# TensorE in the program's order for the mixed batches, with preparation in eight spaced stages, sums in the V products' banks and u transposed early

**Chip, cores, metric.** One Trainium2 chip, one core. The metric is the device time of one launch in microseconds (us), median of several runs. All runs used here were fast (granted TensorE clock 0.98 to 1.00).

## The reference

Hash attention, then a Fourier mixing layer with a two-layer channel network. Cut to what matters:

```python
# q, k, v: (4, 8, 768, 64); proj: (64, 6); w_ch1: (512, 2048); w_ch2: (2048, 512)
q_bucket = sum((q @ proj > 0) * 2 ** arange(6)); k_bucket = ...
scores = where(q_bucket == k_bucket, q @ k.T / 8, -1e9)
x = softmax(scores) @ v                       # -> (4, 768, 512)
u = x + real(fft(fft(x, axis=1), axis=2))
un = (u - mean(u)) / sqrt(var(u) + 1e-6)
out = u + maximum(un @ w_ch1, 0) @ w_ch2
```

## The kernel before

Two heads are worked as a pair n (16 pairs, four per batch). A pair has six key blocks c; one step weighs two query halves g against block c, exponentiates on ACT, masks on DVE, and multiplies the block before by V. The mixing of batch b-1 is a generator of 68 steps (Fourier products cs, A and B; h and o of the channel network), drawn between the attention steps of batch b. Names in the profile: sc scores, oo the product with V, sum the row sums, trq/trk transposed q/k, bits/qb/kb hash bits, un the transposed u.

```python
def pt(shape, name):                   # general tiles: 2 PSUM slots while attention runs
    ...
    return ps_1.tile(shape, F32, tag="ps", name=name)

def prepare(n):                        # yields: after q, after k, after bits, after qb and kb
    ...

def weigh(n, g, c):
    ps = ps_sc.tile([P, 2, 512], F32, tag="sc", name=f"sc{n}_{g}_{c}")
    ...
    for h, rows in enumerate(heads):   # head 0: array rows 0-63, head 1: rows 64-127
        nc.tensor.matmul(ps[:, h, 0:HALF], kt[rows, ks], qt[rows, qs], ...)
    nc.scalar.activation(pk[:, :, 0:HALF], ps[:, :, 0:HALF], AF.Exp, scale=SCALE)
    if kb is not None:
        for h in range(2):
            nc.vector.scalar_tensor_tensor(pk[:, h, 0:HALF], qb[:, h, qs],
                kb[:, h, c : c + 1], pk[:, h, 0:HALF], op0=ALU.is_equal, op1=ALU.mult)
    return pk

def scale(n, oos, accs):
    nc.vector.tensor_copy(vs, oos[0][:, HALF : HALF + 1])
    for g, xg in enumerate(halves):
        nc.scalar.activation(xg, oos[g][:, 0:HALF], AF.Identity, bias=vs)
    for g, xg in enumerate(halves):
        ps = pt([P, HALF], f"sum{n}_{g}")
        ...                            # sum matmuls, then a chain of six DVE operations
# attention of batch 0: every engine keeps the program's order (manual_schedule)
# batches 1 to 3: the framework's scheduler orders every engine by its own time model
```

## Time and profile before

| | us |
|---|---|
| median of 4 runs (lowest to highest) | 1219.55 (1218.6 to 1220.84) |
| span of the profiled run | 1218.6 |
| TensorE busy / idle in the span | 1182.9 / 35.7 |
| DVE, ACT busy | 635.4, 347.0 |

The main lines stand in the prediction below. Read them so: TensorE is busy 97% of the span, so the kernel is as long as TensorE's instruction stream. A record of a 384-column matmul lasts about 490 ns, but the next one starts 322.5 ns later, so "busy" says little. The measure used throughout is the **excess**: the time from each record's start to the next one's, summed over a stretch, less what the same records need at their undisturbed spacing (322.5 ns for 384 columns, 429 for 512, 109 for 128; two halves of the array side by side count half each, the four quarters of bits a quarter each). It holds waits, changes of array shape, half-array matmuls that run without their partner.

### The profile page before, as it was taken

The numbers are of one execution on the slowest core, as the hardware profiler recorded it, in microseconds if no ns is written. First come the engines' busy times: TensorE is split into PE (matmuls) and PEld (weight loads), VectorE is DVE, ScalarE is ACT, GpSimd is POOL, SyncE is SP. The second block draws the span as 40 slices with busy tenths as digits, with TensorE's granted clock in tenths as the row PEclk, the third lists the DMA queues.
The fourth block names the chain that finished last, engine by engine and source line by source line (L and its number), as shares of the span: only waits on it lengthen the run. The fifth ranks groups of instructions, "written<-read, shape, count | busy, mean of one in ns | idle before, by whom it ended". The sixth has DMA issues, their size and how long they took to land. (4 is left out here: it accounts for less than half of the span.)

```text
span 1218.6 us, 11905 instructions
## 1 busy us (share of the span) xinstructions
PE 1182.9 (97%) x4617; PEld 596.3 (49%) x4617; DVE 635.4 (52%) x1202; ACT 347.0 (28%) x612; POOL 57.6 (5%) x128
## 2 busy tenths in 40 slices
PE   7999899999999999999999999999999999999997
PEld 4444364444444456454445445554445546654555
DVE  5889869753374547545446555655445753211110
ACT  7877356532132122222222213222122210000000
POOL 1000001000000010000000010000000000001001
PEclk9999999899999999999999999999999999999999
DMA  9522124201010010100101011010000000000000
GB/s 277 156 65 45 44 87 147 83 14 43 9 26 14 22 38 6 27 13 22 35 22 27 1 31 35 1 39 1 22 17 1 1 10 18 1 1 17 9 9 20
DMA packets 82896, 44.24 MB, mean 36 GB/s; under 512 B 76816, under 2 KB 76944, under 8 KB 82832
## 3 DMA queue, kind: packets, MB, share of 16 engines
q1 hardware_dynamic: 75600, 23.61, 8.0%
q0 software_dynamic: 5664, 19.40, 4.9%
q8 instruction: 38, 0.62, 0.2%
q10 hardware_dynamic: 1568, 0.39, 0.2%
q14 instruction: 26, 0.21, 0.1%
HBM read 37.10 MB, written 6.29 MB: 36 GB/s over the span
## 5 line engine op out<-in xcount | busy, mean ns | idle before, releaser
L1018 PE MATMUL h<-x,w 128*128 128x384 f32 x1024 | 346.3, 494 | 4.8 <-ACT qt L530 2.4
L1049 PE MATMUL o<-w,h 128*128 128x512 f32 (+1 forms) x800 | 339.9, 578 | 0.0
L1018 PEld LDWEIGHTS h<-x,w 128*128 128x128 f32 x1024 | 192.2, 191 | 150.8 <-issue 13.1
L805 DVE SCALAR_TENSOR_TENSOR pk<-qb,kb,pk 128x384 f32<-128x384 bf16 x264 | 151.2, 615 | 184.0 <-ACT pk L802 183.8
L1049 PEld LDWEIGHTS o<-w,h 128*128 128x128 f32 x800 | 148.3, 190 | 169.5 <-issue 160.3
L802 ACT ACTIVATE pk<-sc 128x768 f32<-128x768 f32 x192 | 148.4, 809 | 217.8 <-PE sc L796 178.7
L796 PE MATMUL sc<-qt,kt 64*128 64x384 f32 x768 | 187.3, 507 | 0.0
L816 PE MATMUL oo<-pk,vn 128*64 128x385 f32 (+1 forms) x768 | 145.0, 499 | 0.0
L876 DVE TENSOR_TENSOR acc<-acc,pk 128x768 f32<-128x768 f32 x128 | 120.4, 955 | 9.2 <-ACT pk L802 7.6
L1027 ACT ACTIVATE h<-h 128x384 f32<-128x384 f32 x64 | 31.4, 490 | 281.3 <-PE h L1018 281.2
L1025 DVE TENSOR_SCALAR h<-h 128x384 f32<-128x384 f32 x64 | 35.5, 554 | 143.0 <-PE h L1018 142.9
L796 PEld LDWEIGHTS sc<-qt,kt 64*128 64x128 f32 x768 | 76.6, 186 | 65.9 <-issue 44.3
L1055 DVE SCALAR_TENSOR_TENSOR u<-o,rs,u 128x512 f32<-128x512 f32 (+1 forms) x25 | 18.2, 729 | 165.8 <-PE o L1049 118.3
L816 PEld LDWEIGHTS oo<-pk,vn 128*64 128x64 f32 x768 | 46.6, 136 | 87.3 <-issue 82.5
L1036 ACT COPY u<-un 128x512 f32<-128x512 f32 x24 | 14.0, 586 | 127.3 <-PE un L1034 127.3
L1042 POOL TENSOR_SCALAR rs<-mv 128x1 f32<-128x1 f32 x24 | 7.7, 323 | 593.4 <-DVE mv L1040 588.4
L903 POOL DMA_DIRECT2D out_dram<-u x33 | 19.9, 603 | 316.4 <-DVE u L1055 255.7
L964 PE MATMUL cs<-ch,z 128*128 128x128 f32 (+3 forms) x192 | 31.1, 314 | 2.6 <-DVE kt L528 1.4
L964 PEld LDWEIGHTS cs<-ch,z 128*128 128x128 f32 x192 | 27.5, 191 | 10.1 <-DVE kt L528 3.1
L971 ACT COPY F<-cs 128x257 f32<-128x257 f32 (+1 forms) x32 | 11.1, 374 | 74.7 <-PE cs L964 74.7
L876 DVE TENSOR_TENSOR acc<-pk,pk 128x768 f32<-128x768 f32 x32 | 30.0, 951 | 2.0 <-ACT pk L802 1.7
L828 ACT ACTIVATE x<-oo,vs 128x384 f32<-128x384 f32 x32 | 16.8, 577 | 41.3 <-DVE vs L825 41.3
(107 smaller groups left out, 805.7 us busy)
## 6 DMA issues: line engine op xcount, KB each, us to landing
zraw<-in_moe_w_ch_dram POOLq DMA_DIRECT2D x21, 512.0 KB, 4.5
vn<-in_v_dram SPq DMA_DIRECT2D x32, 192.0 KB, 3.3
qn<-in_q_dram SPq DMA_DIRECT2D x31, 192.0 KB, 3.2
kn<-in_k_dram SPq DMA_DIRECT2D x31, 192.0 KB, 3.2
out_dram<-u POOLq DMA_DIRECT2D x15, 256.0 KB, 2.4
out_dram<-u POOLq DMA_DIRECT2D x18, 128.0 KB, 2.5
fraw<-in_moe_w_ch_dram SPq DMA_DIRECT2D x4, 512.0 KB, 9.2
fraw<-in_moe_w_ch_dram POOLq DMA_DIRECT2D x4, 512.0 KB, 4.5
```

Of the source, the lines that this page charges most:

```text
L796: nc.tensor.matmul(ps[:, h, 0:HALF], kt[rows, ks], qt[rows, qs], start=kb is not None, stop=True,)
L802: nc.scalar.activation(pk[:, :, 0:HALF], ps[:, :, 0:HALF], AF.Exp, scale=SCALE)
L805: nc.vector.scalar_tensor_tensor(pk[:, h, 0:HALF], qb[:, h, qs], kb[:, h, c : c + 1], pk[:, h, 0:HALF], op0=ALU.is_equal, op1=ALU.mult,)
L816: nc.tensor.matmul(oos[g][h * D : (h + 1) * D, 0:w], nat["v", n][:, c, h, :], pk[g][:, h, 0:w], start=(c == 0), stop=(c == NT - 1),)
L876: nc.vector.tensor_tensor(accs[g], first[g][:, :, 0:HALF] if c == 1 else accs[g], new[g][:, :, 0:HALF], op=ALU.add,)
L903: nc.gpsimd.dma_start(out[b, s0 : s0 + 2 * w - 1 : 2, cols], src[at : at + w, cols])
L964: nc.tensor.matmul(ps[:, pc + 2 * lo : pc + 2 * hi - 1 : 2], z[:, cp, pc, par, t * P : (t + 1) * P], ch[:, cp, pc, lo:hi], start=(cp == 0) ...
L1018: nc.tensor.matmul(ps, w1[:, c, fc * P : (fc + 1) * P], x[:, c, g * HALF : (g + 1) * HALF], start=(c == 0), stop=(c == NDC - 1),)
L1025: nc.vector.tensor_scalar(hr, ps, 0.0, None, op0=ALU.max)
L1027: nc.scalar.activation(hr, ps, AF.Relu)
L1049: nc.tensor.matmul(ps, hs[fc][:, j * P : (j + 1) * P], w2[:, fc, cols], start=(fc == 0), stop=(fc == NFC - 1),)
L1055: nc.vector.scalar_tensor_tensor(u[:, cols], ps, rs, u[:, cols], op0=ALU.mult, op1=ALU.add)
```

## The change

The intent: the automatic order pulls the two heads of a score tile apart, and TensorE then runs half empty. So TensorE is tied to the program's order in batches 1 to 3, and the program is rearranged so that this order has few waits: preparation in eight smaller stages with mixing steps between them, the sums' PSUM tiles taken from the V products' two banks so that mixing keeps both general slots, A and B by parity so that a tile is free sooner, u transposed one step before it is needed. Cut to its core (the moved blocks of the batch loop and the new indentation are left out):

```diff
@@ prepare @@
                         ps.rearrange("p c t -> p (c t)"), act,
                     )
+                yield
             ts[nm] = tt
-            yield
             norm(n, io, tn)
...                                   # (the same for bits; and a yield after each qb)
@@ scale @@
-            ps = pt([P, HALF], f"sum{n}_{g}")
+            ps = ps_o.tile([P, HALF], F32, tag="o", name=f"sum{n}_{g}")
@@ attention @@
+    PARTS = 3
+            if c == 0:
+                oos += [ps_o.tile([P, 512], F32, tag="o", ...) for g in range(2)]
             values(n, c, pk, oos)
...
-                if c > 0:
-                    next(ahead, None)
+                for _ in range(PARTS - 1):
+                    yield
+                    if c > 0:
+                        next(ahead, None)
                 yield
+        yield
         while pending:
             finish()
@@ mix @@
-            pa, pb = (pt([P, HALF + 1], f"{nm}{b}_{j}") for nm in "AB")
             for par in range(2):
+                ps = pt([P, 2, NK], f"AB{b}_{j}_{par}")
...                                   # 128 additions of 192 columns for 64 of 384
                 hs.append(hr)
+                if fc == NFC - 2:
+                    nxt = across(b, GT * g)      # transposes u, its mean and variance
                 yield
@@ the batch loop @@
-    LEFT = 8
+    LEFT = 12
-    for b in range(B):
+    with tc.manual_schedule(engines={ET.PE}):
+        for b in range(B):
...
+        roomy[0] = True
+        for _ in range(2 + NT + NDC):
+            next(other)
...                                   # then the check of norms and the load of its flag
```

More of the change, by code (lines that the diff above doesn't have):

```diff
@@ L741, in prepare @@
                         nc.vector.tensor_scalar(bits, bits, BIG, None, op0=ALU.mult)
-                yield
+                    yield
             preps[n] = ts["q"], ts["k"], qk, None
@@ L856, in finish @@
             n, c, pk, oos, accs = pending.pop(0)
+            if c == 0:
+                oos += [
+                    ps_o.tile([P, 512], F32, tag="o", name=f"oo{n}_{g}") for g in range(2)
+                ]
             values(n, c, pk, oos)
@@ L866, in attention @@
             ahead = prepare(n + 1) if n + 1 < NPAIR * B else iter(())
-            oos = [ps_o.tile([P, 512], F32, tag="o", name=f"oo{n}_{g}") for g in range(2)]
+            oos = []
             accs = [wt([P, 2, HALF], F32, "t3", f"acc{n}_{g}", 4) for g in range(2)]
@@ L884, in attention @@
                     next(half, None)
-                if c > 0:
-                    next(ahead, None)
+                for _ in range(PARTS - 1):
+                    yield
+                    if c > 0:
+                        next(ahead, None)
                 yield
+        yield
         while pending:
@@ L945, in fold, with across @@
             yield
+    def across(b, T):
+        x = xs[b]
+        ps = pt([P, NDC, P], f"un{b}_{T}")
+        for c in range(NDC):
+            nc.tensor.transpose(ps[:, c, :], x[:, c, T * P : (T + 1) * P], ident)
+        u = wt([P, DM], F32, "u", f"u{b}_{T}", 2)
+        nc.scalar.copy(u, ps.rearrange("p c n -> p (c n)"))
+        bs = wt([P, 6], F32, "bs", f"bs{b}_{T}")
+        nc.vector.bn_stats(bs, u)
+        mv = wt([P, 2], F32, "mv", f"mv{b}_{T}")
+        nc.vector.bn_aggr(mv, bs)
+        rs = wt([P, 1], F32, "rs", f"rs{b}_{T}")
+        nc.gpsimd.tensor_scalar(rs, mv[:, 1:2], 1e-6, None, op0=ALU.add)
+        nc.gpsimd.tensor_tensor(rs, rs, mhalf, op=ALU.pow)
+        return u, rs
     def mix(b):
@@ L987, in mix @@
         for j in range(NDC):
-            pa, pb = (pt([P, HALF + 1], f"{nm}{b}_{j}") for nm in "AB")
             for par in range(2):
-                cols = slice(par * NK, HALF + 1 if par else NK)
-                for k, ps in enumerate((pa, pb)):
+                ps = pt([P, 2, NK], f"AB{b}_{j}_{par}")
+                n = NK - par
+                cols = slice(par * NK, par * NK + n)
+                for k in range(2):
                     for t in range(2):
                         nc.tensor.matmul(
-                            ps[:, cols], F[:, par, k, t, j * P : (j + 1) * P],
+                            ps[:, k, 0:n], F[:, par, k, t, j * P : (j + 1) * P],
                             sq[:, t, k, cols], start=(t == 0), stop=(t == 1),
                         )
-            for i in range(2):
-                u = x[:, j, i * HALF : (i + 1) * HALF].rearrange("p (r n) -> p r n", r=2)
-                for ps, op in (
-                    (pa, ALU.add), (pb, ALU.subtract if (j < 2) ^ i else ALU.add)
-                ):
-                    if i == 0:
-                        f = ps[:, 0 : 2 * NK - 1]
-                        f = bass.AP(f.tensor, f.offset, [f.ap[0], [NK, 2], [1, HW]])
-                    else:
-                        f = ps[:, HW : HALF + 1]
-                        f = bass.AP(f.tensor, f.offset, [f.ap[0], [HW, 2], [-1, HW]])
-                    nc.vector.tensor_tensor(u, u, f, op=op)
+                for i in range(2):
+                    at = i * HALF + par * HW
+                    u = x[:, j, at : at + HW]
+                    for k in range(2):
+                        f = ps[:, k, 0:HW]
+                        if i == 1:
+                            f = turned(ps[:, k], n - 1, HW)
+                        op = ALU.subtract if k and (j < 2) ^ i else ALU.add
+                        nc.vector.tensor_tensor(u, u, f, op=op)
             yield
@@ L1031, in mix @@
                 T = GT * g + j
-                ps = pt([P, NDC, P], f"un{b}_{T}")
-                for c in range(NDC):
-                    nc.tensor.transpose(ps[:, c, :], x[:, c, T * P : (T + 1) * P], ident)
-                u = wt([P, DM], F32, "u", f"u{b}_{T}", 2)
-                nc.scalar.copy(u, ps.rearrange("p c n -> p (c n)"))
-                bs = wt([P, 6], F32, "bs", f"bs{b}_{T}")
-                nc.vector.bn_stats(bs, u)
-                mv = wt([P, 2], F32, "mv", f"mv{b}_{T}")
-                nc.vector.bn_aggr(mv, bs)
-                rs = wt([P, 1], F32, "rs", f"rs{b}_{T}")
-                nc.gpsimd.tensor_scalar(rs, mv[:, 1:2], 1e-6, None, op0=ALU.add)
-                nc.gpsimd.tensor_tensor(rs, rs, mhalf, op=ALU.pow)
+                u, rs = nxt
                 w = DM // 2 if b == B - 1 and T == NT - 1 else DM
@@ L1053, in mix @@
                         if fc % 4 == 3:
+                            if fc == NFC - 5 and j < GT - 1:
+                                nxt = across(b, T + 1)
                             yield
@@ L1084, in _main @@
         for i, _ in enumerate(attention(0)):
-            if i % 5 < 4:
+            if i % PARTS == PARTS - 1 and i // PARTS % 5 < 4:
                 next(other, None)
@@ L1095, in _main @@
             nc.scalar.copy(means[-1][1], average(f))
-    for b in range(B):
-        if b > 0:
-            wait = 0
-            if b == 1:
-                next(other)
-                next(other)
-                wait = 2
-            steps, done = NPAIR * NT - wait, 2 if b == 1 else 0
-            for i, _ in enumerate(attention(b), 1):
-                if b == 1 and i == 2:
-                    for f, avg in means:
-                        centre(f, avg)
-                while done * steps < (MIX - LEFT) * (i - wait):
-                    next(other)
-                    done += 1
-        if b == B - 1:
-            roomy[0] = True
-            ms = const.tile([P, 3], F32, tag="ms", name="ms")
-            nc.vector.tensor_reduce(ms[:, 0:2], norms, axis=AX.X, op=ALU.max)
-            nc.vector.tensor_reduce(ms[:, 2:3], strange, axis=AX.X, op=ALU.max)
-            ps = pt([1, 3, P], "norms_t")
-            for io in range(3):
-                nc.tensor.transpose(ps[:, io, :], ms[:, io : io + 1], ident)
-            mt = const.tile([1, 5], F32, tag="mt", name="mt")
-            nc.vector.tensor_reduce(mt[:, 0:3], ps, axis=AX.X, op=ALU.max)
-            nc.vector.tensor_tensor(mt[:, 3:4], mt[:, 0:1], mt[:, 1:2], op=ALU.mult)
-            nc.vector.tensor_scalar(
-                mt[:, 4:5], mt[:, 3:4], (SAFE / SCALE) ** 2, None, op0=ALU.is_gt
-            )
-            fl = const.tile([1, 1], I32, tag="fl", name="fl")
-            nc.vector.scalar_tensor_tensor(
-                fl, mt[:, 2:3], 0.0, mt[:, 4:5], op0=ALU.is_gt, op1=ALU.max
-            )
-            large = nc.values_load(fl[0:1, 0:1], min_val=0, max_val=1)
@@ new lines, in _main @@
+    with tc.manual_schedule(engines={ET.PE}):
+        for b in range(B):
+            if b > 0:
+                wait = 0
+                if b == 1:
+                    next(other)
+                    next(other)
+                    wait = 2 * PARTS
+                steps, done = NPAIR * NT * PARTS - wait, 2 if b == 1 else 0
+                for i, _ in enumerate(attention(b), 1):
+                    if b == 1 and i == wait:
+                        for f, avg in means:
+                            centre(f, avg)
+                    goal = (MIX - LEFT) * (i - wait) / steps
+                    if i > NPAIR * NT * PARTS:
+                        goal = MIX - LEFT + 4
+                    while done < goal:
+                        next(other)
+                        done += 1
+            for _ in other:
+                pass
+            other = mix(b)
+            if b == 0:
+                other = after(2 + NT, other, weights(w2, moe_w_ch2))
+        roomy[0] = True
+        for _ in range(2 + NT + NDC):
+            next(other)
+        ms = const.tile([P, 3], F32, tag="ms", name="ms")
+        nc.vector.tensor_reduce(ms[:, 0:2], norms, axis=AX.X, op=ALU.max)
+        nc.vector.tensor_reduce(ms[:, 2:3], strange, axis=AX.X, op=ALU.max)
+        ps = pt([1, 3, P], "norms_t")
+        for io in range(3):
+            nc.tensor.transpose(ps[:, io, :], ms[:, io : io + 1], ident)
+        mt = const.tile([1, 5], F32, tag="mt", name="mt")
+        nc.vector.tensor_reduce(mt[:, 0:3], ps, axis=AX.X, op=ALU.max)
+        nc.vector.tensor_tensor(mt[:, 3:4], mt[:, 0:1], mt[:, 1:2], op=ALU.mult)
+        nc.vector.tensor_scalar(
+            mt[:, 4:5], mt[:, 3:4], (SAFE / SCALE) ** 2, None, op0=ALU.is_gt
+        )
+        fl = const.tile([1, 1], I32, tag="fl", name="fl")
+        nc.vector.scalar_tensor_tensor(
+            fl, mt[:, 2:3], 0.0, mt[:, 4:5], op0=ALU.is_gt, op1=ALU.max
+        )
+        large = nc.values_load(fl[0:1, 0:1], min_val=0, max_val=1)
@@ L1135, in _main @@
         for _ in other:
             pass
-        other = mix(b)
-        if b == 0:
-            other = after(2 + NT, other, weights(w2, moe_w_ch2))
-    for _ in other:
-        pass
     return large
```

## The prediction

> **What bounds the kernel now.** I read the page first, then the busy time in stretches, then TensorE's timeline, then the list of waits.
>
> ```profile
> PE 1182.9 (97%) x4617; PEld 596.3 (49%) x4617; DVE 635.4 (52%) x1202; ACT 347.0 (28%) x612; POOL 57.6 (5%) x128
> PE   7999899999999999999999999999999999999997
> PEclk9999999899999999999999999999999999999999
> ```
>
> TensorE is busy 97% of the span at an almost full granted clock (mean 0.994); nothing else comes near. So the end is set by the length of TensorE's instruction stream, and idle time can give back at most 1218.6 - 1182.9 = 35.7 us. About 8 us of that is the start, before the first loads have landed, and 7.7 us the last store after the last matmul; neither is touched.
>
> ```profile
> 0.00:150.70 150.70, 133.72 (x713) 61.29 (x713) 123.54 (x228) 101.65 (x187) 6.49 (x28) 0.99 0.43 117
> 150.70:441.60 290.90, 285.86 (x1085) 140.84 (x1085) 166.34 (x321) 98.27 (x173) 19.74 (x35) 0.99 0.17 48
> 441.60:737.40 295.80, 292.68 (x1121) 143.24 (x1120) 159.48 (x300) 70.10 (x118) 10.77 (x21) 1.00 0.09 22
> 737.40:998.00 260.60, 257.73 (x1022) 128.25 (x1021) 143.93 (x263) 61.90 (x103) 7.00 (x15) 1.00 0.06 15
> 998.00:1218.60 220.60, 212.87 (x683) 122.67 (x680) 42.07 (x91) 15.06 (x32) 13.57 (x29) 0.99 0.03 10
> ```
>
> These stretches (length, then busy time of PE, PEld, DVE, ACT, POOL) are cut where each batch's first mixing product (cs) runs: roughly attention of batch 0; attention 1, 2 and 3 each mixed with the Fourier and channel work of the batch before; and batch 3's mixing alone. In the three middle stretches (847 us) TensorE is idle only 11 us. But busy time counts a matmul's whole record, so it hides a stream that is spread out. What is spread shows in the timeline:
>
> ```profile
> 491.19 1.56 PE L796 MATMUL sc<-qt,kt 64*128 64x384 f32 x8
> 492.68 1.51 PE L816 MATMUL oo<-pk,vn 128*64 128x385 f32 x8
> 494.02 1.46 PE L833 MATMUL sum<-acc,ones 128*64 128x384 f32 x8
> ...
> 515.43 0.91 PE L796 MATMUL sc<-qt,kt 64*128 64x384 f32 x2
> 516.27 1.51 PE L816 MATMUL oo<-pk,vn 128*64 128x385 f32 x8
> 517.71 0.87 PE L708 MATMUL trk<-ident,kn 128*128 128x128 f32 x6
> 518.51 0.91 PE L796 MATMUL sc<-qt,kt 64*128 64x384 f32 x2
> ```
>
> A score tile (sc) is two heads, each on 64 rows of the array, each f32 product recorded as two passes: four records. At 491.19 two whole tiles, eight records, take 1.49 us until the next kind starts: the heads run side by side. At 515.43 one head's two records take 0.84 us alone, and the other head follows at 518.51, again alone. The program issues both heads together; the automatic order pulled them apart. Batch 0's attention, which already keeps program order, shows almost only whole groups.
>
> I took TensorE's records of the three middle stretches in order of start. Spacing inside a run of one shape is constant: 322.5 ns for 384 columns, 429 for 512, 109 for 128, and half of 322.5 per record where two halves of the array run together. Summed at that spacing (sc and oo counted as paired) the three stretches need 747 us; they take 847. The 100 us of excess are 11 us of waits and 89 us in which a record is "busy". There are 344 runs of one array shape. Excess per run (median): full array 0.20 us; oo 0.15; bits 0.14; qb/kb 0.10; sc 0.20 with whole tiles, 0.52 with a head alone. By kind: full 123 runs, 28.1 us; sc 115 runs, 46.1; oo 72 runs, 11.0; the rest 3.6. Of the 115 sc runs 66 contain a head alone.
>
> **What the Trainium skill says.** "TensorE: Matmul & The Clock Gate", Part 3, The mechanism: matmuls on different row groups of the array run concurrently, and matmuls keep strict issue order. The trace agrees: paired records start 7 ns apart, and a head whose partner comes later does not catch up. "TensorEngine Tiling (Array Packing)", Key Properties: changing the tiling mode drains TensorE. The trace puts a number on it: about 0.1 us at the end of a run and 0.05 to 0.1 at the next one's start. "Perfetto Trace Analysis", Identifying the Most-Contended Engine: matmul busy share does not tell how near a kernel is to its limit, because matmuls are pipelined; here 97% busy hides the 89 us.
>
> **The change, part by part.**
>
> *TensorE in program order for batches 1 to 3.* Every step then is: two whole score tiles, the V product, then mixing and preparation. 24 steps times 3 batches = 72 rounds, each with one sc run, one oo run and at least one full-array run. Preparation adds runs: eleven pairs (n = 5 to 15) use bits, qb twice and kb, each of another array shape. With the mixing steps between them (56 over 72 places, 0.78 a place) I count about 34 more full runs and 33 short ones. Sum: sc 72 x 0.20 = 14.5; oo 72 x 0.15 = 11; full 106 x 0.21 = 22.3; bits 11 x 0.14 = 1.5; qb and kb 33 x 0.10 = 3.2; together 52.5 us in place of 88.8. **Saved: 36 us**, all on the bounding engine. The 11 us of waits belong to the old order and go too; new ones come below.
>
> *Sums in the V products' two banks.* The sum matmul follows the V product at once (316 ns after its last record in nearly all pairs). It now needs a bank that is read first by DVE (vs, 0.15) and by ACT (x, 0.58).
>
> ```profile
> 493.05 1.15 DVE L805 SCALAR_TENSOR_TENSOR pk<-qb,kb,pk 128x384 f32<-128x384 bf16 x2 [3.70 <-ACT pk L802]
> 494.11 0.15 DVE L825 COPY vs<-oo 128x1 f32<-128x1 f32 x1
> ...
> 494.30 1.05 ACT L828 ACTIVATE x<-oo,vs 128x384 f32<-128x384 f32 x2 [0.58 <-DVE vs L825]
> ```
>
> Here the first of ACT's two ends at 494.88; the sum started at 494.02. It would have started at 494.93, 0.9 us late; the second sum then finds its bank free. Where no mask work stands before vs (at 995.0, for one) it is about 0.45 us. Twelve pairs: **about +9 us**. In batch 0 the vector engine is full of weight conversion: for the first pair vs came at 43.06 and the sum had run at 41.73, so there the wait is 1.5 to 2.2 us, and the reciprocal chain on DVE is delayed with it. Four pairs, nearly 8 us; DVE and TensorE are both near their limits there, so I take **+6 us**.
>
> *Preparation in eight stages.* No matmul more or less. It puts a transposition of 0.65 us between mixing steps that share two PSUM slots: the mixing step after it needs the slot of the one before it, whose eviction (0.49 on ACT, 0.55 on DVE) hardly fits into 0.65 us, and DVE's mask and accumulate burst in a step (4 x 0.56 + 2 x 0.95 = 4.1 us) sometimes stands before it. I take 0.4 us a pair for twelve pairs: **+5 us**.
>
> *A and B by parity.* The same matmuls; 128 vector additions of 192 columns at about 0.35 us (the z rows with 192 columns took 352 ns) for 64 of 0.55: DVE +10 us in all. Per step of A and B DVE then needs 2.8 us against TensorE's 2.6; with the mask work beside it DVE leads for two attention steps in each of three batches, and TensorE in strict order can't go past: **+5 us**. Alone at the end (batch 3) the lag stays below the 1.9 us for which the first three quarters of an h product run: 0.
>
> *u transposed early.* Moves 12.2 us of transpositions by one step; they waited for nothing: 0. *The flag (norms) later, in TensorE's order:* one short chain, **+1 us**. First h products after A and B, bits before qb where no mixing step falls between: **+2 us**.
>
> Sum: -36 - 11 + 9 + 6 + 5 + 5 + 1 + 2 = -19; 1219.3 - 19 = **1200 us**, a gain of 1.6%.
>
> **Rivals.**
>
> *Order pays in full.* If DVE takes vs before the masks and the slots come free in time, the new waits shrink to some 8 us in all: 1219 - 47 + 8 = about 1180. For it: slices at 52% DVE and 28% ACT leave room, and constants such as twelve steps kept back look tried out. Against: the dependency of the sum on ACT cannot be ordered away.
>
> *New waits eat the gain.* Strict order with two slots stalls at every preparation stage (48 transpositions, 0.6 us each, as in the waits of h for "ACT qt" now: 2.4 us in 4 times) and 2 us per sum: 29 + 24 + 10 = 63 us for 47 saved, about 1235. For it: the automatic order exists to fill such holes. Against: batch 0, in program order, had about 9 us of waits after its start. Something half-way, near 1212, is likelier.
>
> *Vector engine becomes the bound in cs and A/B stages.* It was 22 of 30 us busy at 450 to 480. 15 us more instead of my 5: 1210.
>
> **Range and chances.** The 36 us are counted from measured runs and I trust them to 5 us. The 28 us of new waits may be 12 to 40. So 1184 to 1212. A gain over 2% needs less than 1194.9, 5 us below my figure with a spread of about 10: 0.30. Slower by 2% needs 1243.7, 72 us of new waits: 0.04. Within 2%: 0.66.
>
> **What would show it.** Right: in the middle stretches every sc run has eight f32 records and about 72 sc runs are left; the mean time from sc to the next start per tile falls; sum now waits for "ACT x", about 0.9 us, 16 times; the last 212 us stretch is unchanged. Wrong: heads still apart (then the order was not the cause); sum not waiting; waits of h or o for "ACT h", "DVE h" or "DVE acc" in tens of us; batch 0 longer by over 10 us.

## The result

The changed kernel takes 1246.79 us (4 runs, 1244.88 to 1248.58) against 1219.55: ratio 1.0222, 95% interval 1.0204 to 1.0241. It is **slower by 2.2%**; forecast were 1200 us and 1184 to 1212. (A ratio here is the mean time of one kernel's fast runs over that of the other's of the same rounds, so not quite the ratio of the medians.) The output is correct.

The changed kernel's page, to set beside the first fence of the prediction:

```profile
span 1242.9 us, 11964 instructions
PE 1163.0 (94%) x4617; PEld 586.4 (47%) x4617; DVE 650.3 (52%) x1266; ACT 345.7 (28%) x612; POOL 54.6 (4%) x128
PE   7988887999999998999998999899999999999997
```

The same 4617 matmuls are *busy* 20 us less and *idle* 80 us in place of 36. Its stretches, cut at the first cs of each batch as before (length; busy PE, PEld, DVE, ACT, POOL; clock; DMA):

```profile
0.00:156.30 156.30, 134.07 (x708) 59.92 (x708) 123.71 (x228) 102.27 (x187) 6.47 (x28) 0.99 0.41 113
156.30:456.80 300.50, 282.30 (x1088) 139.28 (x1088) 167.84 (x334) 96.31 (x172) 18.04 (x37) 0.98 0.16 46
456.80:756.30 299.50, 283.18 (x1122) 139.29 (x1120) 164.74 (x316) 69.49 (x119) 9.88 (x22) 1.00 0.09 22
756.30:1046.70 290.40, 277.51 (x1084) 137.31 (x1083) 161.26 (x310) 63.64 (x106) 9.49 (x20) 1.00 0.06 14
1046.70:1242.90 196.20, 185.91 (x620) 110.60 (x618) 32.74 (x78) 13.97 (x30) 10.70 (x23) 0.99 0.03 10
```

Idle time stands now in every stretch with attention: 18 us in the second, where there were 5. (The lengths of the last two can't be compared: some 27 us of o products of batch 2 moved from the last to the one before it.) From here on the middle is cut from batch 0's first cs to the last oo record, in every kernel.

Who TensorE waited for (total us, times, longest), the changed kernel:

```profile
PE sum L834 <- ACT x L829: 17.1, 16, 2.5
PE AB L1023 <- DVE x L1036: 9.3, 7, 3.4
PE h L1045 <- DVE h L1052: 6.2, 6, 1.8
PE cs L993 <- DVE kt L528: 5.1, 3, 2.8
...
PE AB L1023 <- DVE F L1006: 3.2, 2, 1.6
PE trq L708 <- ACT qt L530: 3.1, 2, 1.6
PE h L1045 <- DVE fl L1164: 2.6, 1, 2.6
PE trq L708 <- DVE h L1052: 2.3, 3, 1.3
```

Two of these in the timeline. First a sum; then an h product between two transpositions:

```profile
505.97 1.56 PE L797 MATMUL sc<-qt,kt 64*128 64x384 f32 x8
507.46 1.51 PE L817 MATMUL oo<-pk,vn 128*64 128x385 f32 x8
509.71 1.51 PE L834 MATMUL sum<-acc,ones 128*64 128x384 f32 x8 [0.74 <-ACT x L829]
511.15 2.20 PE L1045 MATMUL h<-x,w 128*128 128x384 f32 x6
...
534.34 1.82 DVE L885 TENSOR_TENSOR acc<-acc,pk 128x768 f32<-128x768 f32 x2
534.84 0.49 PE L708 MATMUL trk<-ident,kn 128*128 128x128 f32 x3
536.08 0.55 DVE L1052 TENSOR_SCALAR h<-h 128x384 f32<-128x384 f32 x1
536.69 2.85 PE L1045 MATMUL h<-x,w 128*128 128x384 f32 x8 [1.36 <-DVE h L1052]
```

At 505.97 the score tiles are whole, eight records at a time, in every step: this part works as forecast. But the sum starts 1.22 us after the last V record in place of 0.32. At 534 the vector engine accumulates until 536.1, only then evicts the h tile before the transposition, and the next h product, which needs that slot, stands still 1.36 us although its operands have long been there. An idle interval also costs more than its idle time: the record before it covers some 0.17 us in which the next could have started (0.91 us lost at the sum, 0.74 of them idle), and the first record after it takes about 0.1 us more.

One more thing is in these traces. The granted clock falls to 0.50 for stretches of about 3.4 us, and the same 16 matmuls then take 1.6 us more:

```profile
182.50 4.47 PE L1023 MATMUL AB<-sq,F 128*128 128x193 f32 x16 [3.39 <-DVE x L1036]
...
197.92 2.88 PE L1023 MATMUL AB<-sq,F 128*128 128x193 f32 x16
```

The middle of the changed kernel has three such stretches (at 182.4, 202.9 and 230.2 us), each at the end of a wait or within 1 us of it. That the wait brings the lower clock is not shown by any run. Estimated as half of TensorE's busy time in such stretches, they cost the middle about 5 us in the changed kernel, 3 in the kernel before, 15 in order_only, 8.5 in sums_back and stages_paired, 3.4 in tiles_glued and none in attention_glued. They are a small part of the 25 us lost (2 us), but not of order_only's loss. They also differ between runs of one kernel: the changed kernel read 0.994 at 1244.88 us and 0.991 at 1248.58.

### The profile page after: what moved, and what is told of

It is laid out like the page before. It is cut to its first block, busy times and chain, and to the rows that moved or that the text cites. A ratio compares the mean times of both kernels' runs of the same rounds, so it can differ in the third digit from the quotient of the medians.

```text
span 1242.9 us, 11964 instructions
## 1 busy us (share of the span) xinstructions
PE 1163.0 (94%) x4617; PEld 586.4 (47%) x4617; DVE 650.3 (52%) x1266; ACT 345.7 (28%) x612; POOL 54.6 (4%) x128
## 5 line engine op out<-in xcount | busy, mean ns | idle before, releaser
L1045 PE MATMUL h<-x,w 128*128 128x384 f32 x1024 | 354.3, 497 | 15.4 <-DVE h L1052 6.2
L797 PE MATMUL sc<-qt,kt 64*128 64x384 f32 x768 | 152.8, 501 | 0.2 <-DVE qb L528 0.2
L1052 DVE TENSOR_SCALAR h<-h 128x384 f32<-128x384 f32 x64 | 35.5, 554 | 124.7 <-PE h L1045 124.6
L797 PEld LDWEIGHTS sc<-qt,kt 64*128 64x128 f32 x768 | 67.3, 186 | 53.8 <-issue 35.5
L968 DVE BATCH_NORM_STATS2 bs<-u 128x6 f32<-128x512 f32 x24 | 16.6, 692 | 112.3 <-ACT u L966 112.3
L1023 PE MATMUL AB<-sq,F 128*128 128x193 f32 (+1 forms) x256 | 47.4, 339 | 12.4 <-DVE x L1036 9.3
L1023 PEld LDWEIGHTS AB<-sq,F 128*128 128x128 f32 x256 | 42.9, 195 | 18.4 <-issue 8.8
L1036 DVE TENSOR_TENSOR x<-x,AB 128x192 f32<-128x192 f32 x128 | 39.3, 348 | 10.0 <-PE AB L1023 9.1
L834 PE MATMUL sum<-acc,ones 128*64 128x384 f32 x128 | 24.5, 503 | 17.1 <-ACT x L829 17.1
```

The costliest lines, as they stand in the source:

```text
L1023: nc.tensor.matmul(ps[:, k, 0:n], F[:, par, k, t, j * P : (j + 1) * P], sq[:, t, k, cols], start=(t == 0), stop=(t == 1),)
L1036: nc.vector.tensor_tensor(u, u, f, op=op)
L1045: nc.tensor.matmul(ps, w1[:, c, fc * P : (fc + 1) * P], x[:, c, g * HALF : (g + 1) * HALF], start=(c == 0), stop=(c == NDC - 1),)
L1052: nc.vector.tensor_scalar(hr, ps, 0.0, None, op0=ALU.max)
```

## The experiments

Theory A: the strict order itself makes the new waits, because TensorE can no longer go past a tile whose eviction stands in DVE's queue. Theory B (rival): the parts that came with it make them, and the order alone would gain. A question beside both: are heads apart really the cost that I read?

The accounts of all runs. "Runs" are stretches of one array shape in the middle; "alone" are score records without partner, then V records without partner; "idle" is TensorE's idle time in the middle; the excess is given for batch 0's attention / the middle / the end.

| run | median us | ratio to before (95%) | runs | alone | idle us | excess us |
|---|---|---|---|---|---|---|
| before | 1219.6 to 1220.6 | 1 | 342 | 160, 0 | 11.0 | 28.1 / 99.7 / 0.6 |
| changed | 1246.8 | 1.0222 (1.0204 to 1.0241) | 280 | 0, 0 | 47.2 | 34.4 / 114.7 / 3.9 |
| auto_order | 1232.0 | 1.0093 (1.0076 to 1.0110) | 385 | 88, 64 | 8.6 | 36.1 / 103.3 / 1.0 |
| order_only | 1268.3 | 1.0391 (1.0374 to 1.0409) | 232 | 0, 0 | 72.1 | 29.2 / 143.8 / 4.1 |
| sums_back | 1236.4 | 1.0127 (1.0109 to 1.0145) | 280 | 0, 0 | 43.2 | 27.8 / 112.4 / 5.3 |
| stages_paired | 1254.2 | 1.0272 (1.0242 to 1.0303) | 263 | 0, 0 | 53.9 | 34.7 / 122.3 / 3.9 |
| ab_old | 1247.3 | 1.0222 (1.0206 to 1.0237) | 280 | 0, 0 | 45.9 | 36.1 / 113.6 / 5.6 |
| h_on_act | 1240.4 | 1.0172 (1.0151 to 1.0192) | 280 | 0, 0 | 42.2 | 34.4 / 109.4 / 5.6 |
| no_masks (wrong result) | 1231.8 | 1.0096 (1.0081 to 1.0111) | 280 | 0, 0 | 31.5 | 35.5 / 100.4 / 3.9 |
| three_eased | 1231.0 | 1.0089 (1.0073 to 1.0104) | 280 | 0, 0 | 37.1 | 29.0 / 104.3 / 5.1 |
| heads_glued | 1195.7 | 0.9791 (0.9771 to 0.9811) | 340 | 0, 12 | 8.5 | 27.8 / 75.2 / 0.6 |
| tiles_glued | 1193.1 | 0.9775 (0.9762 to 0.9789) | 300 | 0, 28 | 11.2 | 27.5 / 74.3 / 0.6 |
| attention_glued | 1186.0 | 0.9718 (0.9704 to 0.9731) | 292 | 0, 0 | 9.2 | 28.6 / 64.8 / 0.6 |
| attention_glued_act | 1186.8 | 0.9726 (0.9712 to 0.9739) | 292 | 0, 0 | 9.2 | 27.8 / 66.3 / 0.6 |

The excess accounts for the result: the changed kernel has 6.3 us more in batch 0, 15.0 more in the middle and 3.3 more at the end, together 24.6; the spans differ by 24.3.

**1. The order taken out of the change.**

```diff
-    with tc.manual_schedule(engines={ET.PE}):
+    if True:
         for b in range(B):
```

> The changed kernel with TensorE's order in batches 1 to 3 left to the automatic scheduler again; all else as changed. Theory A (strict order itself makes the new waits): the waits of the middle stretches fall from about 62 us to under 25, while its order has 393 runs of one array shape against 288 and some 41 heads alone, about 25 us more of those; so near 1220 to 1230 us. Theory B (the other parts, sums in the V banks, A and B by parity, eight stages, make the waits): stays at or above 1245 us, because the runs get dearer and the waits stay.

Measured 1232.0 us: 15 us faster than the changed kernel, still 12 slower than before, and 2 us above what theory A expected. The idle time of the middle is gone (47.2 to 8.6 us), so the strict order does make the waits: theory A. What remains over before is 8.0 us in batch 0 (the sums' banks, see 3) and 3.6 in the middle. The latter can be summed roughly: 72 score records fewer alone (-11.6 us at 161 ns), 64 V records alone (+10.3), 43 more runs (+7 at about 0.17) and 2.4 us less idle.

**2. The order alone, on the kernel before.**

```diff
-    for b in range(B):
+    with tc.manual_schedule(engines={ET.PE}):
+      for b in range(B):
```

> The kernel before with only TensorE's program order for batches 1 to 3. 244 runs against 343 and no head alone: about 40 us less excess between runs. Theory A: the new waits exceed that, 1240 us or more, because whole preparation steps and mixing steps share two slots with nothing between. Theory B: the order alone gains, 1180 to 1200 us.

1268.3 us, 4% slower: theory B falls, the order alone loses 48 us, of which the half clock above is about 12 (15 less the 3 of the kernel before). Its waits (total, times, longest):

```profile
PE h L1018 <- ACT qt L530: 13.8, 5, 5.4
PE kb L770 <- ACT qb L530: 8.9, 10, 0.9
PE trq L708 <- ACT qt L530: 7.2, 3, 2.4
PE trk L708 <- DVE kt L528: 6.3, 3, 2.1
```

I read this so: whole preparation steps take both general slots, and the mixing behind them waits for their evictions. The change's other parts together win back 21 of the 48 us; which of them does is not shown (see 4).

**3. The sums' banks.**

```diff
-            ps = ps_o.tile([P, HALF], F32, tag="o", name=f"sum{n}_{g}")
+            ps = pt([P, HALF], f"sum{n}_{g}")
```

> The changed kernel with the sums back in the general banks. If the 16 waits of sum for ACT x (7 us in the middle, 8 us in batch 0) are a loss by themselves: 12 to 15 us faster, near 1233 us. Rival: the sums then hold both general slots over the reciprocal chain on DVE and the next mixing step waits as long: within 5 us of 1246.

1236.4 us, 10 us faster than the changed kernel; I had expected 12 to 15. The split is instructive: batch 0 gains 6.6 us of excess, the middle only 2.3, although the 12 sums of the middle no longer wait for ACT. In their place stand waits that the changed kernel does not have:

```profile
PE AB L1023 <- DVE rt L840: 3.3, 2, 2.4
...
PE h L1045 <- DVE rt L840: 2.3, 6, 0.4
```

The sums now hold the general slots until DVE has read them (rt), and the mixing waits: in the middle the rival of this run is partly right; in batch 0, where no mixing wants the slots, the theory is. Two cautions: the two profiled runs differ by 7.6 us, not 10, and the half clock takes about 3.5 us more from the middle of sums_back than from that of the changed kernel, so 2.3 understates what the waits alone gave back.

**4. Eight stages, spaced or not.**

```diff
-                for _ in range(PARTS - 1):
+                for part in range(PARTS - 1):
                     yield
-                    if c > 0:
+                    if c > 0 and part == 0:
                         next(ahead, None)
+                        next(ahead, None)
```

> The changed kernel with the eight preparation stages run two at a time, with no mixing step between the two: as before the change. 275 runs against 288, 2 us for that. If spacing the stages is what makes strict order bearable (order_only is 22 us slower than the whole change), 8 to 20 us slower than 1247, with waits of h, kb and trq for ACT qt and qb as in order_only. Rival: within 4 us.

1254.2 us, 7 us slower, a little under the range expected; the four runs spread from 1248.6 to 1257.7, with clocks from 0.995 to 0.986. But the edit does not restore the kernel before: it pairs bits with the first qb, which stood a mixing step apart there, and the new wait is that one, not those of h and kb that I had expected:

```profile
PE qb L761 <- DVE bt L753: 11.5, 11, 1.9
```

Idle time in the middle is 53.9 us; without this wait it is 42.4, less than the 47.2 of the changed kernel. So the run shows what bits beside qb costs. That spacing the transpositions helps is not shown, and which parts of the change (stages, mixing steps kept back, u early) win the 21 us over order_only was not taken apart.

**5. The vector engine's burst of masks.**

```diff
-        if kb is not None:
+        if False:
             for h in range(2):
                 nc.vector.scalar_tensor_tensor(
```

> The changed kernel without the mask products (wrong result on purpose): 264 vector operations, 150 us, gone, matmuls and order the same. If strict order waits because evictions stand behind the vector engine's burst of masks, the waits of AB, h, trq and cs for DVE fall by over half and the sums' waits from 0.74 to 0.23 us: 15 to 30 us faster than 1247. Rival (the waits are the bare eviction latency of two slots): less than 8 us faster.

1231.8 us: 15 us faster, the lower edge of what was expected. Idle time in the middle falls from 47.2 to 31.5 us. The masks are thus behind a third of the idle time; two thirds stay with DVE's 150 us of masks gone altogether. The expectation held only in part: the waits of h for DVE h fell by over half (6.2 to 2.7 us), but those of AB for DVE x (9.3 to 6.4) and of cs for DVE kt (5.1 to 4.2) did not.

**6. A and B as before.** The edit puts back the two tiles of 385 columns and the 64 additions (the minus lines of the diff above).

> The changed kernel with A and B as before the change (two tiles of 385 columns, 64 vector additions of 0.55 us in place of 128 of 0.35). If A and B by parity cost strict order what I put on them (DVE 10 us more): 3 to 8 us faster than 1247. Rival: by parity each tile is free sooner, so without it strict order waits longer: slower by 3 us or more (order_only shows A and B waiting about 11 us).

1247.3 us, no difference (0.5 us). Neither guess shows as a net effect. The two may cancel: A waits for DVE x 6.3 us where AB waited 9.3, a wait of h for DVE rc of 2.5 us is new, and the granted clock was lower (0.989 to 0.990 against 0.991 to 0.994).

**7. All h evictions on ACT.**

```diff
-                if fc % 2:
-                    nc.vector.tensor_scalar(hr, ps, 0.0, None, op0=ALU.max)
-                else:
-                    nc.scalar.activation(hr, ps, AF.Relu)
+                nc.scalar.activation(hr, ps, AF.Relu)
```

> The changed kernel with all 128 evictions of h on ACT, in place of every other one on DVE. Same matmuls, same order, right result. If h and the transpositions wait because h's eviction stands behind masks and accumulation in DVE's queue, the waits of h and trq for DVE h (8.5 us idle, some 11 us in all) vanish and ACT brings at most 3: 6 to 12 us faster than 1247. Rival (bare latency of two slots): within 3 us.

1240.4 us, 6.4 faster, as expected at the lower edge. The waits for "DVE h" (8.5 us) are gone from its list; those for "ACT h" rise from 1.9 to 4.5 us, within the 3 us more that I had allowed:

```profile
PE h L1045 <- ACT h L1051: 1.9, 7, 0.4
PE trk L708 <- ACT h L1051: 1.6, 1, 1.6
PE trq L708 <- ACT h L1051: 1.0, 4, 0.3
```

So most of this wait was DVE's queue, as at 534 to 536 above, and not the two slots' bare latency.

**8. Three together, order kept.** Edits 3, 6 and 7.

> The changed kernel, strict order kept, with sums back in the general banks, A and B as before and h on ACT. If the waits are separate they add: 10 from the sums, 6 to 12 from h, and what ab_old shows: about 1225 to 1230. If strict order only moves a wait to the next tile: 1233 us or more. In either case it stays above attention_glued (1186).

1231.0 us, just above the 1225 to 1230 expected. The single effects add: -10.4, +0.5 and -6.4 make -16.3; measured -15.8. Still 37 us of idle time stay in the middle, and the kernel is slower than before.

**9. Heads tied, all else automatic.** On the kernel *before*:

```diff
-        for h, rows in enumerate(heads):
-            nc.tensor.matmul(...)
+        with tc.manual_schedule(engines={mybir.EngineType.PE}):
+            for h, rows in enumerate(heads):
+                with tc.high_priority() if h else ExitStack():
+                    nc.tensor.matmul(...)
```

The inner region fixes the issue order of the two matmuls; the high priority makes the scheduler take the second at once when the first is out. The first keeps its priority, so the pair goes where the head would have gone.

> The kernel before, automatic order, but the second head's score product is tied to the first (issue order and high priority), so no head runs alone; runs of one shape stay at 341 (343). If a head alone costs what I read (160 records at 161 ns more): 20 to 26 us faster, 1193 to 1200 us. Rival (heads apart fill holes, so tying them brings the waits back): within 6 us of 1219.

1195.7 us, **24.9 us faster than before** (ratio 0.9791, interval 0.9771 to 0.9811). The excess of the middle falls by 24.5 us; 160 records at 161 ns are 25.8, less 12 V records that now stand alone (1.9), make 23.9. Runs and idle time hardly move. The cost of a head alone is thus shown, and it can be won back without the order.

**10. The whole attention step tied.** tiles_glued ties all four score products of a step; attention_glued also the four V products to one another:

```diff
-            values(n, c, pk, oos)
+            with tc.manual_schedule(engines={mybir.EngineType.PE}):
+                values(n, c, pk, oos)     # all but the first at high priority
...
-                new = [weigh(n, g, c) for g in range(2)]
+                with tc.manual_schedule(engines={mybir.EngineType.PE}):
+                    new = [weigh(n, g, c) for g in range(2)]   # the same
```

> The kernel before, automatic order, with all four score products of a step tied (both heads of both tiles): 301 runs of one shape against 341 in heads_glued, no head alone. 40 runs fewer at 0.15 to 0.2 us: 6 to 8 us faster than heads_glued, near 1188 us, if the automatic order still fills the waits. Rival: a longer tied block leaves fewer places to fill and both score banks are asked for at once, waits eat it: within 4 us of 1196 or slower.

> As tiles_glued, and the four V products of a step tied to one another too: 293 runs. 8 runs fewer: 1 to 2 us faster than tiles_glued; rival: no difference or slower by new waits.

tiles_glued takes 1193.1, only 2.5 us less than heads_glued where I expected 6 to 8; this is the rival's range, and the single runs of the two overlap (heads_glued 1192.1 to 1196.4, tiles_glued 1192.5 to 1194.4). The 40 runs saved (about 6 us) are partly paid back, by V records alone (28 in place of 12, 2.6 us) and 2.7 us more idle time. attention_glued puts the V products together too and takes **1186.0 us**, 2.8% faster than before and 4.9% faster than the change; I had expected 1 to 2 us of this step and got 7, because I had counted its runs and not its lone V records (28 x 161 ns = 4.5 us). Its profiled run also has no half clock in the middle, which is an estimated 3.4 us of the 9.5 between the two profiles. Its timeline:

```profile
481.32 1.56 PE L797 MATMUL sc<-qt,kt 64*128 64x384 f32 x8
482.81 8.01 PE L1022 MATMUL h<-x,w 128*128 128x384 f32 x24
490.75 1.51 PE L818 MATMUL oo<-pk,vn 128*64 128x385 f32 x8
492.19 0.87 PE L708 MATMUL trq<-ident,qn 128*128 128x128 f32 x6
493.00 1.56 PE L797 MATMUL sc<-qt,kt 64*128 64x384 f32 x8
```

Blocks of eight, whole, and no wait: the scheduler has put one transposition stage between V and scores, and three h tiles where they fit. The number of runs in the middle is almost that of the changed kernel (292 and 280), and no record is alone in either; the excess is 64.8 and 114.7 us. That is the price of the strict order with everything that came with it, with the runs' structure held.

**11. The fastest with h on ACT.**

> The fastest so far (attention_glued, 1186) with all evictions of h on ACT. Automatic order already fills waits (9 us idle in the middle): within 3 us of 1186. Rival: h evictions still cost it hidden waits: 4 to 8 us faster.

1186.8 us, no difference. Where the order is free, h's evictions on DVE do no harm that can be seen; the same edit gave 6.4 us under strict order.

## Why the prediction was wrong

- *"TensorE is the bound; the stream is spread by heads apart and by changes of shape"*: right. heads_glued gives 24.5 us for the heads, attention_glued 34.9 us of excess for heads and runs.
- *"Saved: 36 us"*: right as a size. All score tiles are whole; 280 runs at the same medians (full 105 x 0.20, sc 69 x 0.20, oo 70 x 0.15, the rest 37 for 4 to 5 us) are about 50 us; I had said 52.5.
- *"The 11 us of waits belong to the old order and go too"* and the new waits of +9, +5, +5 and +2 us in the middle: **this failed.** The middle's excess is 114.7; less the 50 of runs that leaves about 65 us of waits where I summed 21. Term by term, as the lost spacing of the records, classed by what each waited for: the twelve sums 10.7 (said 9); cs, A and B and the first h about 23 (said 5, and a part of 2); slots shared by h, o and preparation about 30 (said 5). About 5 of these 65 us are the half clock, which the prediction did not reckon with: some 3.3 in the second figure and 1.7 in the third.
- *"0.4 us a pair"* for preparation is the worst-sized term. I reckoned that an eviction nearly fits into the 0.65 us of a transposition, and that DVE's burst stands in front of it "sometimes". When it does, it costs 1 us and more (h for DVE h: 6 times, 6.2 us idle), and smaller waits for ACT qt, DVE kt and the evictions of u come on top. h_on_act and no_masks show DVE's queue to be the cause for 6 and 15 us. The rest is neither the masks' nor h's evictions' doing, so its cause stays open; whether a third general slot would remove it is open, none was tried.
- *A and B, +5*: the waits at A and B are there (9.3 and 3.2 us idle), but ab_old shows no net cost of the parity form. The step's cause is not confirmed.
- *Sums, +6 in batch 0*: measured +6.3, and sums_back takes it away again. In the middle the estimate of 9 was near (10.7), but sums_back wins back only 2.3 us of it, with about 3.5 us more of half clock: most of the rest returns as waits for the general slots.
- *The flag, +1*: the end's excess rose by 3.3 us. One wait of 2.6 us of h for "DVE fl": in strict order TensorE loads the flag before it may go on.
- *Rival "new waits eat the gain"*: I put 63 us of new waits and 1235 us to it and called it less likely than 1212. It was the right one in its outcome (about 65 in the middle, 6 and 3 outside). That 65 is so near to 63 is luck: its 24 us for the sums were 10.7, and its 10 us for the remainder stood against about 23 at cs, A, B and the first h. My argument against it, that batch 0 had few waits in program order, was weak: batch 0 has no mixing that shares the two slots. And my argument for the change, constants that "look tried out", is no evidence.

The Trainium skill's statements used in the prediction held: paired records start 7 ns apart, and each change of shape costs time. What I took from no page and no view was how much the automatic order hides: 11 us of idle time in the kernel before told me what was left after hiding, not what there was to hide.

## What to carry to other kernels

A scheduler's order can have one defect worth mending and many merits that do not show in a profile, since a hidden wait leaves no line. Tie together only the instructions whose nearness pays (here two half-array matmuls, then eight) and leave the rest free; try the order alone before building on it. In a strict order a shared buffer or the queue of an evicting engine can become part of the critical path, so size those waits from the queue's work ahead of each eviction, not from the idle time of the old order.

## What the Trainium skill lacked or had wrong

- "TensorEngine Tiling (Array Packing)", Key Properties, says that a change of tiling mode drains TensorE, without a size. Here a run of one shape costs 0.20 us (full array, or two halves of its rows) or 0.15 us (two halves of its columns) beyond its streaming time; 342 runs in the middle of the kernel before.
- "TensorE: Matmul & The Clock Gate", Part 3, gives the gain of packed tiles, but not that an automatic order can separate them. Issued apart, a half-array record takes 161 ns more here; 160 of them were 24.5 us (heads_glued).
- "Perfetto Trace Analysis", Identifying the Most-Contended Engine, rightly warns of matmul busy share (97%, 94% and 97% for 1219, 1247 and 1186 us). The LDWEIGHTS busy share that it names instead does rank the three rightly (48.9%, 47.2% and 49.4%), but with loads of nearly equal time (596.3, 586.4 and 584.9 us) it is little more than the span turned round, and it shows no place where time is lost. The spacing of starts against its undisturbed value does (excess 128, 153 and 94 us).
- No page gives it as a rule for reading waits that a wait of TensorE costs more than the idle time shown; "TensorE: Matmul & The Clock Gate", Part 2, comes near it where it says that a matmul standing alone cannot hide its drain. Here 0.91 us were lost for 0.74 idle at the sums.
